# Two range checks moved from VectorE to ScalarE, and a re-planned order, in a fused attention and MLP kernel on one core

## The chip, the cores and the metric

One core of one Trainium2 chip runs one program. The metric is the device time of one execution in microseconds (us), taken as the median of several; lower is better. Engine names are those of the profile: PE (TensorE, its weight loads apart as PEld), DVE (VectorE), ACT (ScalarE), POOL (GpSimd), SP (the queue that issues the transfers).

## The reference

Three parts follow each other: a gated linear attention with complex gates, an RMS norm with a SiLU-gated MLP, and a second MLP with softplus. Cut to what matters (shapes: 4 x 8 heads x 768 steps x 48; 3072 tokens of 384; hidden widths 1536 and 2048):

```python
mag = np.sqrt(a_re * a_re + a_im * a_im)
scale = np.minimum(mag, 0.999) / (mag + 1e-06)
...
for t in range(S):
    new_re = ar * S_re - ai * S_im
    new_im = ar * S_im + ai * S_re
    kv = np.einsum('bhd,bhe->bhde', k[:, :, t], v[:, :, t])
    S_re, S_im = (new_re + kv, new_im)
    y[:, :, t] = np.einsum('bhd,bhde->bhe', q[:, :, t], S_re)
...
xn = x / rms * rms_g
g = xn @ w_gate
silu = g * (1.0 / (1.0 + np.exp(-g)))
return (silu * (xn @ w_val) @ w_out)
...
h = x @ w_in
g = np.maximum(h, 0.0) + np.log1p(np.exp(-np.abs(h)))
return (g @ w_out)
```

## The kernel before, in words

**Attention.** The 768 steps are cut into 6 chunks of 128 for each of 4 batches: 24 units. For each unit the gates' magnitudes and angles are formed (`squares`, `logs`, `mags`, `tangent`, `trigs`, `psi`, `frac`), q and k are scaled and rotated (`q_scaled`, `k_scaled`, `rotated`, tiles `pc` and `ps`), written to memory and read back in another layout (`relayout`, tiles `rot` and `QK`), and PE makes the products within a chunk (`gram`, L597; `ys`, L640 and L643; `kv`, L663; all in PSUM tiles `patt`). Two transposes and the RMS norm (`norm`, L710 to L714) give the unit's part of the first MLP's input, split into a rounded part `xh` and a rest `xl` (`x_evac`, L738 for `xl`). Most of this work is elementwise on tiles of 128x384, on DVE, ACT and POOL.

**The MLPs.** Each float32 product is made of three, rounded times rounded and the two cross terms, so each weight too is a pair (`w1h`, `w1l`). The first MLP works through 6 tiles of 512 tokens (4 units each) and 12 blocks of the hidden width: two input products (`a_in`, PSUM tile `hp`), SiLU on ACT (`sil`), a product with the gate on DVE, the split into `ph` and `pl` (L866), and an output product (`a_out`, PSUM tile `op`); all matmuls stand in L815. `ph` and `pl` have one buffer each, so a block's `ph` can be written only after the block before has been multiplied out. The second MLP has the same form (`b_in`, `b_act`, `b_out`).

**The weights** arrive as 64-bit numbers, in pieces of 128x384 (36 for the first MLP, 32 for the second). `w_split` makes float32 of each: ACT takes the high word's magnitude (L790) and the low word's bits (L792), DVE clamps the magnitude into a range (L795) and puts the bits together (L797 to L803), then the piece is split in two (`whi`, L808).

**Checks.** The fast path needs a gate's real part over a bound: L413 clamps it on DVE and accumulates the least value into `am`. Such checks meet in `flags` near the end of the attention; a flag that is set runs a general kernel instead.

**Order.** The program has no loop at run time. `Plan` holds every step with its cost on each engine that may do it (`CHOICE`), a position plus a correction from tables (`EARLY`, `LEAD`), and places them greedily on model clocks; the order of each engine's instructions is what comes out, and each engine then runs its list in that order. 150 matmuls without use (`keep_warm`, L1035) fill PE's gaps early on. The first `a_in` needs `xh` and `xl` of units 0 to 3.

Of the kernel before, what the change touches and what calls it, by code (L numbers as in the profile page):

```python
# [1301 lines left out]
```

## Time and profile before

| what | value |
|---|---|
| runs | 1105.39, 1106.09, 1109.11 us; median 1106.09 |
| the profiled execution's own time | 1107.23 us |
| its span, first to last instruction | 1105.4 us |
| PE, DVE, ACT, POOL busy | 1038.9, 781.7, 696.4, 167.8 us |
| first matmul of the first MLP | about 123.5 us after the start |

Busy times are of one execution. PE's is a modelled one, since matmuls overlap; an engine's busy share over the whole span mixes stages that have different limits, so the rows below are cut by stage.

### The profile page before, as it was taken

How to read it: one execution, taken by the hardware profiler on the slowest of the kernel's cores; microseconds unless marked ns; L12 is line 12 of the kernel's file. 1: busy time of each engine (PE TensorE's matmuls, PEld its weight loads, DVE VectorE, ACT ScalarE, POOL GpSimd, SP SyncE). 2: the span in 40 equal slices, each digit the busy share in tenths (PEclk: the TensorE clock that was granted, in tenths of full speed). 3: DMA queues.
4: the chain of work that ended last, by engine and by line, in shares of the span. 5: the costliest groups of instructions: out<-in, count | busy, mean ns of one | idle time of the engine just before them, and what ended most of it. 6: DMA issues, size and time to landing. Idle time of an engine off the chain costs nothing.

```text
span 1105.4 us, 15919 instructions
## 1 busy us (share of the span) xinstructions
PE 1038.9 (94%) x5694; PEld 873.5 (79%) x5694; DVE 781.7 (71%) x1541; ACT 696.4 (63%) x1275; POOL 167.8 (15%) x208
## 2 busy tenths in 40 slices
PE   0694899999999999999999999999999999999997
PEld 0693787888887888888888888888888888888886
DVE  7999999988999889898343298598445454544443
ACT  7797787688788788787422265596544454444543
POOL 1132312222334225232010000000000000000000
PEclk9996799999999999999999999999999999999999
DMA  6577556644565454453220054242001010000000
GB/s 197 153 198 173 164 151 168 157 137 112 143 138 136 121 146 108 139 142 93 79 73 20 20 152 115 72 137 63 29 1 58 1 58 1 10 29 1 29 1 32
DMA packets 98344, 103.84 MB, mean 94 GB/s; under 512 B 5456, under 2 KB 82640, under 8 KB 98256
## 3 DMA queue, kind: packets, MB, share of 16 engines
q1 hardware_dynamic: 98256, 102.73, 34.2%
q8 instruction: 47, 0.77, 0.3%
q14 instruction: 41, 0.34, 0.1%
HBM read 74.33 MB, written 28.39 MB: 93 GB/s over the span
## 4 chain that ended last, share of the span: by engine, by line
PE 74%; DVE 12%; ACT 6%; DMA 5%; issue 2%; POOL 1%; SPq 0%; ACTq 0%; DVEq 0%; POOLq 0%
PE hp L815 29%; PE op L815 27%; PE hq L815 7%; PE patt L597 3%; DMA QK<-rot 2%; PE patt L640 2%; PE op L1035 2%; PE patt L663 2%; ACT L1106 1%; DMA wst<-w 1%; DMA rot<-ps 1%; PE patt L643 1%; DVE pl L866 1%; PE patt L616 1%; DVE AT L607 1%
## 5 line engine op out<-in xcount | busy, mean ns | idle before, releaser
L815 PE MATMUL hp<-xh,w1h 128*128 128x512 f32 x516 | 207.4, 402 | 0.0
L815 PE MATMUL hp<-xl,w1h 128*128 128x512 f32 x516 | 201.9, 391 | 0.7 <-DVE xl L738 0.7
L815 PE MATMUL hp<-xh,w1l 128*128 128x512 f32 x516 | 202.0, 391 | 0.0
L815 PEld LDWEIGHTS hp<-xh,w1l 128*128 128x128 f32 x516 | 97.3, 188 | 21.0
L815 PEld LDWEIGHTS hp<-xl,w1h 128*128 128x128 f32 x516 | 97.5, 189 | 19.7 <-DVE xl L738 1.2
L815 PEld LDWEIGHTS hp<-xh,w1h 128*128 128x128 f32 x516 | 97.5, 189 | 19.0 <-issue 0.3
L962 DVE SCALAR_TENSOR_TENSOR be<-hp,be 128x512 f32<-128x512 f32 x58 | 40.1, 691 | 96.2 <-ACT be L959 96.2
L957 ACT ACTIVATE be<-hp 128x512 f32<-128x512 f32 x58 | 34.8, 600 | 104.6 <-PE hp L815 104.4
L863 DVE TENSOR_TENSOR sil<-sil,hp 128x512 f32<-128x512 f32 x72 | 49.0, 681 | 56.9 <-PE hp L815 53.4
L815 PE MATMUL op<-ph,w1h 128*128 128x512 f32 x216 | 87.0, 403 | 0.0
L815 PE MATMUL op<-pl,w1h 128*128 128x512 f32 x216 | 84.7, 392 | 0.2 <-DVE pl L866 0.2
L815 PE MATMUL op<-ph,w1l 128*128 128x512 f32 x216 | 84.4, 391 | 0.0
L372 ACT CAST ph<-sil 128x512 fp32r<-128x512 f32 x51 | 31.7, 621 | 67.5 <-PE op L815 37.1
L962 DVE SCALAR_TENSOR_TENSOR be<-hq,be 128x512 f32<-128x512 f32 x38 | 26.3, 692 | 63.8 <-ACT be L959 63.8
L866 DVE TENSOR_TENSOR pl<-sil,ph 128x512 fp32r<-128x512 f32 x72 | 56.0, 778 | 21.8 <-ACT ph L372 17.6
L965 DVE TENSOR_TENSOR bpl<-be,bph 128x512 fp32r<-128x512 f32 x96 | 66.3, 691 | 4.0 <-POOL bph L376 1.2
L597 PE MATMUL patt<-QK 96*128 96x128 f32 x384 | 52.2, 290 | 16.2 <-DMA QK<-rot 11.1
L597 PEld LDWEIGHTS patt<-QK 96*128 96x128 f32 x384 | 50.1, 203 | 20.5 <-issue 8.5
L1106 ACT ACT_TABLE_LOAD x51 | 65.4, 1283 | 0.7
L957 ACT ACTIVATE be<-hq 128x512 f32<-128x512 f32 x38 | 22.8, 600 | 67.5 <-PE hq L815 67.5
L855 ACT ACTIVATE sil<-hp 128x512 f32<-128x512 f32 x72 | 43.2, 600 | 32.4 <-PE hp L815 32.1
L958 ACT ACTIVATE be<-be 128x512 f32<-128x512 f32 x96 | 61.0, 635 | 3.0
(183 smaller groups left out, 2606.5 us busy)
## 6 DMA issues: line engine op xcount, KB each, us to landing
wst<-w SPq DMA_DIRECT2D x68, 384.0 KB, 3.2
QK<-rot SPq DMA_DIRECT2D x96, 192.8 KB, 4.9
rot<-pc SPq DMA_DIRECT2D x24, 385.5 KB, 3.3
rot<-ps SPq DMA_DIRECT2D x24, 385.5 KB, 4.2
aa<-aa SPq DMA_DIRECT2D x24, 384.0 KB, 4.2
qk<-qk SPq DMA_DIRECT2D x24, 384.0 KB, 5.3
v<-vv SPq DMA_DIRECT2D x24, 192.0 KB, 5.0
x2d<-ev SPq DMA_DIRECT2D x18, 256.0 KB, 2.6
```

The lines of the kernel that those rows point to most:

```text
L372: act.copy(out=dst, in_=src)
L597: pe.matmul(T(g)[:, i * C:(i + 1) * C], lhsT=T(q)[:, i, C:2 * C], rhs=T(q)[:, i, 0:C], start=True, stop=True)
L640: pe.matmul(o(h), lhsT=T(v)[:, h * D:h * D + 64], rhs=T(a)[:, h, :], start=True, stop=ch == 0)
L815: pe.matmul(o, lhsT=w[:, wcol + k * 128:wcol + (k + 1) * 128], rhs=x[:, k, 0:n], start=first and i == 0, stop=last and i == len(m) - 1)
L855: op(ACT, c_drain(n), lambda: act.activation(out=T(s)[:, 0:n], in_=T(g)[:, 0:n], func=AF.Silu), r=[g], w=[s, "silu"], prio=p, table="silu")
L863: op(DVE, c_dve(n), lambda: dve.tensor_tensor(out=T(s)[:, 0:n], in0=T(s)[:, 0:n], in1=T(v)[:, 0:n], op=ALU.mult), r=[v], w=[s], prio=p)
L866: flex("plo", "tt", n, lambda e: e.tensor_tensor(out=T(pl)[:, 0, 0:n], in0=T(s)[:, 0:n], in1=T(ph)[:, 0, 0:n].bitcast(F32), op=ALU.subtrac ...
L957: act.activation(out=T(e), in_=T(h), func=AF.Abs)
L958: act.activation(out=T(e), in_=T(e), func=AF.Exp, scale=-1.0)
L962: op(DVE, c_dve(512), lambda: dve.scalar_tensor_tensor(out=T(e), in0=T(h), scalar=0.0, in1=T(e), op0=ALU.max, op1=ALU.add), r=[h], w=[e], ...
L965: flex("bplo", "tt", 512, lambda x: x.tensor_tensor(out=T(pl)[:, 0], in0=T(e), in1=T(ph)[:, 0].bitcast(F32), op=ALU.subtract), r=[e, ph], ...
L1106: P.emit(lambda tab: tab in TABLES and act.preload_act_table_set(TABLES[tab]))
```

## The change

1. `squares`: the clamp of the gates' real part on DVE (L413) goes. Instead ACT forms relu(bound - value) and adds it up (`asum`), into the tile that the square of the real part then overwrites; a sum over zero sets the flag.
2. `w_split` for the first MLP's 36 pieces: DVE's clamp (L795) goes. ACT's magnitude step now adds up the magnitudes too, and a new ACT step (`w_small`) adds up relu(2^-15 - magnitude), writing into the place of the piece's later `w1h`. Both sums are compared in `flags`. The second MLP's pieces keep the clamp.
3. `flags` has 8 more small instructions on DVE; `floor` becomes one column, read 128 times over.
4. The planner: other waiting times from one engine to the next (`SEEN`), some other costs, `SLACK` 529 instead of 14578 (how much later than its best engine a step may end), other engines to choose from (`CHOICE`), and new numbers in `EARLY` and `LEAD`. Nearly every row of every engine's list moves.

```diff
+SEEN = {"dve": 115.0, "act": 140.0, "pe": 200.0, "pool": 140.0, "sp": 200.0, None: 200.0}
...
-    "bphi": "dp adp", "bplo": "p d", "add": "p d",
+    "bphi": "dp ad", "bplo": "d d", "add": "dp dp",
...
-    "whi": "ad adp", "wlo": "d d", "phi": "a ap", "plo": "d d", "oev": "a ad", "x2hi": "p adp", "x2lo": "d dp",
...
+    "whi": "adp ad", "wlo": "dp d", "phi": "a ad", "plo": "dp p", "oev": "a ad", "x2hi": "p dp", "x2lo": "dp dp",
...
-SLACK = 14578.0
+SLACK = 529.0
...
-                    ready[j] = max(ready[j], done + (GAP if self.ops[j][0][0][0] == e else 200.0))
+                    ready[j] = max(ready[j], done + (GAP if self.ops[j][0][0][0] == e else SEEN[e]))
...
 def c_pool2(n):
-    return 182 + 2.0 * n
+    return 260 + 2.0 * n
...
-        op(DVE, c_dve(N) + 60, lambda: dve.tensor_scalar(
-            out=T(k)[:, 0], in0=T(k)[:, 0], scalar1=AR_MIN, scalar2=None, op0=ALU.max, op1=ALU.min,
-            accum_out=am[:, u:u + 1]), w=[(k, 0), ("am", u)], prio=p)
+        op(ACT, c_act(N) + 50, lambda: act.activation(
+            out=T(a), in_=T(k)[:, 0], func=AF.Relu, scale=-1.0, bias=bias[:, 4:5], accum_out=am[:, u:u + 1]),
+            r=[(k, 0)], w=[a, ("am", u)], prio=p, name="asum")
...
-        op(POOL, 750, rstd, w=[ss], prio=p)
+        op(POOL, 1100, rstd, w=[ss], prio=p)
...
+    def w_abs(key, k, dst, dk, p):
+
+        if key[0] == "w2":
...
+        i = key[1]
+        op(ACT, c_act(PW, 0.5) + 50, lambda: act.activation(
+            out=dst(), in_=T(k)[:, :, 1].bitcast(F32), func=AF.Abs, accum_out=wm[:, 0, i:i + 1]),
+            r=[k], w=[dk, ("wb", i)], prio=p, name="w_abs")
+        op(ACT, c_act(PW) + 50, lambda: act.activation(
+            out=T(w1k[i // 3][0])[:, i % 3 * PW:(i % 3 + 1) * PW], in_=dst(), func=AF.Relu,
+            scale=-1.0, bias=bias[:, 5:6], accum_out=wm[:, 1, i:i + 1]),
+            r=[dk], w=[(w1k[i // 3][0], i % 3 * PW), ("ws", i)], prio=p, name="w_small")
...
-            op(ACT, c_act(PW, 0.5), lambda: act.activation(out=af(), in_=T(k)[:, :, 1].bitcast(F32), func=AF.Abs),
-               r=[k], w=[a], prio=p)
+            w_abs(key, k, af, a, p)
...
-            op(DVE, c_fast(PW), lambda: dve.tensor_scalar(
-                out=af(), in0=af(), scalar1=W_BIG, scalar2=2.0 ** -15, op0=ALU.min, op1=ALU.max), w=[a], prio=p, port=True)
...
+        if wide:
+            for i, limit, at in ((0, W_BIG, ALU.is_lt), (1, 0.0, ALU.is_le)):
+                dve.tensor_scalar(out=wm[:, i], in0=wm[:, i], scalar1=limit, scalar2=None, op0=at)
+                dve.tensor_reduce(out=fl[:, 3:4], in_=wm[:, i], axis=AX.X, op=ALU.min)
+                dve.tensor_scalar(out=fl[:, 3:4], in0=fl[:, 3:4], scalar1=1.0, scalar2=None, op0=ALU.is_lt)
+                dve.tensor_tensor(out=fl[:, 0:1], in0=fl[:, 0:1], in1=fl[:, 3:4], op=ALU.add)
...
-        op(DVE, 1500, flags, w=keys, prio=p)
+        op(DVE, 2300, flags, w=keys, prio=p)
```

Three places of the new order follow; the line numbers of the changed kernel are a little higher (L817 is L797 of before, L715 is L710, L886 is L866, L379 and L377 are L374 and L372, L883 is L863).

DVE at its first weight pieces (`ev` holds a piece's magnitude, `wst` its raw words, `aa` the gates), before:

```order
L795 TENSOR_SCALAR ev<-ev 128x384
L797 TENSOR_SCALAR ev<-ev 128x384
L800 SCALAR_TENSOR_TENSOR ev<-wst,ev 128x384
L795 TENSOR_SCALAR ev<-ev 128x384
L803 SCALAR_TENSOR_TENSOR ev<-ev 128x384
L797 TENSOR_SCALAR ev<-ev 128x384
```

and now:

```order
L817 TENSOR_SCALAR ev<-ev 128x384
L820 SCALAR_TENSOR_TENSOR ev<-wst,ev 128x384
L823 SCALAR_TENSOR_TENSOR ev<-ev 128x384
L817 TENSOR_SCALAR ev<-ev 128x384
L820 SCALAR_TENSOR_TENSOR ev<-wst,ev 128x384
```

Each piece has four rows here before, three now, and its first row now follows ACT's new step instead of ACT's magnitude step.

ACT around the norm square of unit 3, the last unit that the first MLP tile needs (`yx,ss<-patt` is that square, `wm` and `am` are the sums), before:

```order
L790 ACTIVATE ev<-wst 128x384
L792 ACTIVATE ev<-wst,bias 128x384
L366 ACTIVATE C<-C,mhalf 128x384
L790 ACTIVATE ev<-wst 128x384
L792 ACTIVATE ev<-wst,bias 128x384
L372 COPY yx<-patt 128x512
L386 ACTIVATE B<-aa 128x384
L710 ACTIVATE yx,ss<-patt 128x384
```

and now:

```order
L795 ACTIVATE ev,wm<-wst 128x384
L814 ACTIVATE ev<-wst,bias 128x384
L377 COPY yx<-patt 128x512
L798 ACTIVATE w1h_678,wm<-ev,bias 128x384
L715 ACTIVATE yx,ss<-patt 128x384
L391 ACTIVATE B<-aa 128x384
L377 CAST xh<-patt 128x3x128
L418 ACTIVATE A,am<-aa,bias 128x384
```

A piece has three rows on ACT instead of two (the third, L798, stands just ahead of the norm square), and the unit's gate sum (L418) is a row of ACT's.

POOL in the middle of the attention (`ph`, `pl` belong to the first MLP, `pc`, `qk`, `A`, `T`, `C` to the attention), before:

```order
L706 TENSOR_SCALAR ss<-ss 128x1
L708 TENSOR_TENSOR ss<-ss,mhalf 128x1
L418 TENSOR_TENSOR A<-A,B 128x384
L376 TENSOR_SCALAR pc<-e_all 128x3
L376 TENSOR_SCALAR ph<-sil 128x512
L376 TENSOR_SCALAR ps<-e_all 128x3
L376 TENSOR_SCALAR ph<-sil 128x512
L567 TENSOR_TENSOR pc<-qk,G 128x3x256
```

and now:

```order
L373 TENSOR_SCALAR T<-T 128x384
L474 TENSOR_TENSOR T<-aa,Z 128x384
L886 TENSOR_TENSOR pl<-sil,ph 128x512
L557 TENSOR_TENSOR qk<-qk,F 128x384
L498 TENSOR_TENSOR A<-B,C 128x384
L373 TENSOR_SCALAR C<-C 128x384
L886 TENSOR_TENSOR pl<-sil,ph 128x512
```

POOL now subtracts for `pl` (66 of its 72, all 72 of which were DVE's) and no longer makes `pc` (17, now DVE's); `ph` left POOL for DVE and ACT.

## Rows read from the trace of the kernel before

**Rows 1.** The page, parts 1 and 2: busy times, and PE's 40 slices.

```profile
PE 1038.9 (94%) x5694; PEld 873.5 (79%) x5694; DVE 781.7 (71%) x1541; ACT 696.4 (63%) x1275; POOL 167.8 (15%) x208
PE   0694899999999999999999999999999999999997
```

**Rows 2.** Windows by stage: length; PE, PEld, DVE, ACT, POOL busy; clock; DMA share, GB/s.

```profile
0.00:123.50 123.50, 69.06 (x548) 65.22 (x548) 110.74 (x253) 95.38 (x195) 29.84 (x35) 0.88 0.66 176
123.50:229.40 105.90, 103.26 (x630) 86.36 (x630) 101.16 (x219) 84.45 (x170) 24.92 (x26) 0.98 0.61 157
229.40:333.60 104.20, 103.99 (x653) 87.50 (x652) 94.44 (x178) 88.45 (x163) 30.86 (x43) 1.00 0.55 134
333.60:441.50 107.90, 106.73 (x694) 89.97 (x693) 94.06 (x181) 85.38 (x160) 43.59 (x47) 1.00 0.49 131
441.50:544.30 102.80, 102.20 (x634) 86.04 (x633) 81.30 (x149) 75.45 (x135) 24.21 (x32) 1.00 0.36 103
...
640.00:720.00 80.00, 80.00 (x354) 66.24 (x354) 60.71 (x134) 47.22 (x84) 1.75 (x3) 1.00 0.39 112
720.00:1092.00 372.00, 372.00 (x1642) 308.02 (x1642) 201.94 (x365) 194.19 (x321) 5.67 (x10) 1.00 0.10 31
```

**Rows 3.** The chain of waits, 0 to 140 us: start, length, what.

```profile
12.68 0.47 DVE w1l L808
...
17.75 0.28 DVE ev L795
...
26.91 0.27 DVE w1h L374
...
33.52 0.87 DVE pc L567
...
78.58 0.41 ACT A L386
...
93.18 0.52 ACT T L478 x2
...
104.61 6.64 DMA QK<-rot
...
124.42 0.47 DVE xl L738
```

**Rows 4.** Groups by line and shape: busy us and mean ns, then idle before.

```profile
L795 DVE TENSOR_SCALAR ev<-ev 128x384 f32<-128x384 f32 x68 | 26.1, 386 | 3.0 <-ACT ev L790 3.0
L413 DVE TENSOR_SCALAR_CACHE_REDUCE aa<-aa 128x384 f32<-128x384 f32 x24 | 12.9, 539 | 2.2 <-DMA aa<-aa 2.2
L478 ACT ACTIVATE T<-T 128x384 f32<-128x384 f32 x24 | 12.5, 522 | 0.4
L478 ACT ACTIVATION_READ_ACCUMULATOR T<-T 128x1 f32 x24 | 4.6, 191 | 0.0
```

**Rows 5.** The timeline around the flags, 586 to 588 us: start, length, what, idle before.

```profile
586.62 0.23 DVE L988 TENSOR_REDUCE fl<-e_all 128x1 f32<-128x72 f32 x1
...
587.50 0.17 DVE L996 MEMSET floor<- 128x128 f32 x1
```

**Rows 6.** The same stretch on PE.

```profile
587.81 0.35 PE L998 MATMUL patt<-fl,floor 128*128 128x3 f32 x2 [0.34 <-DVE floor L996]
```

**Rows 7.** Groups by line and shape: POOL's two-input work, and the split of the gated product.

```profile
L567 POOL TENSOR_TENSOR pc<-qk,G 128x768 f32<-128x768 f32 x17 | 32.3, 1898 | 28.5 <-ACT G L459 16.1 <-ACT pc L372 9.6 <-issue 2.5
...
L545 POOL TENSOR_TENSOR qk<-qk,E 128x384 f32<-128x384 f32 x8 | 17.2, 2151 | 46.4 <-DMA qk<-qk 29.4 <-DVE E L488 17.0
L418 POOL TENSOR_TENSOR A<-A,B 128x384 f32<-128x384 f32 x15 | 17.1, 1141 | 44.2 <-ACT A L386 41.0 <-DVE pl L866 3.1
```

**Rows 8.** The same view, where `ph` is made.

```profile
L372 ACT CAST ph<-sil 128x512 fp32r<-128x512 f32 x51 | 31.7, 621 | 67.5 <-PE op L815 37.1 <-DVE sil L863 29.1 <-DVE ev L797 0.6
```

**Rows 9.** The chain of waits past the attention.

```profile
600.54 2.04 PE hp L815 x9
602.58 2.04 PE op L815 x9
```

More of the change, by code (lines that the diff above doesn't have):

```diff
@@ new lines @@
+    "masked.dve": {0: -291, 1: -147, 2: -114, 3: -293, 4: 101},
+    "norm.act": {0: 400, 1: -226, 2: -473, 3: 340, 4: 281}, "norm.dve": {0: 32, 1: -139, 2: -192, 3: 321, 4: -347},
+    "norm.pool": {0: 199, 1: -29, 2: 477, 3: 46, 4: -36},
+    "nw1": {-1: 463, 0: 232, 1: -201, 2: 499, 3: -234, 4: -215},
+    "nw2": {-1: -328, 0: -73, 1: -268, 2: -453, 3: -307, 4: -374},
+    "nw3": {-1: -9, 0: -522, 1: 555, 2: -208, 3: -353, 4: 385}, "phi": {0: 142}, "plo": {0: 80},
+    "psi.dve": {0: 154, 1: 315, 2: 510, 3: 598, 4: 569}, "qe": {0: -453, 1: 492, 2: -180, 3: 385, 4: -476},
@@ new lines @@
+    "w_load.sp": {0: -315, 1: 129, 2: 392, 3: -44, 4: 491, 5: -219},
+    "w_small": {0: -397, 1: 145, 2: -12, 3: -329, 4: -96, 5: 214},
+    "w_split.act": {0: 255, 1: 482, 2: 106, 3: -480, 4: 380, 5: 309},
+    "w_split.dve": {0: 423, 1: 350, 2: 387, 3: -22, 4: 205, 5: -22},
+    "whi": {0: 179, 1: 445, 2: -139, 3: -158, 4: 47, 5: -302},
+    "wlo": {0: 369, 1: 204, 2: -291, 3: -243, 4: -514, 5: 75},
+    "x_evac.dve": {0: 342, 1: -300, 2: 227, 3: 95, 4: 101}, "x_tr.pe": {0: -404, 1: 95, 2: -342, 3: -163, 4: 68},
@@ new lines @@
+    "b_act.act": 431, "b_act.dve": -370, "b_in.pe": 318, "b_out.pe": -360, "back": -5, "begin_b.None": 151,
+    "bphi": -332, "bplo": 44, "carried.dve": -449, "carry": 119, "eend": -418, "evac.sp": -197, "flags.dve": 290,
+    "frac.dve": -83, "gram.pe": -389, "k_nat.pe": 184, "k_scaled.dve": 183, "kf": 301, "knev": -59, "kv.pe": -508,
+    "load_a.sp": -328, "load_consts.sp": -93, "load_qk.sp": 252, "load_v.pool": 345, "load_v.sp": 153, "logs2": -123,
+    "logs3": -40, "mags.dve": 198, "masked.dve": -165, "norm.act": -309, "norm.dve": 198, "norm.pool": -313,
@@ L324, in fused_kernel @@
     cst = ctx.enter_context(tc.tile_pool(name="cst", bufs=1, side="left"))
-    bias = cst.tile([128, 4], F32, name="bias")
+    bias = cst.tile([128, 8], F32, name="bias")
     mlp = ctx.enter_context(tc.tile_pool(name="mlp", bufs=1, side="left"))
@@ L342, in fused_kernel @@
     g_bc = ac.tile([128, DM], F32, name="g_bc")
-    floor = ac.tile([128, 128], F32, name="floor")
+    floor = edge.tile([128, 8], F32, name="floor")[:, 0:1]
     later_steps = ac.tile([128, N], F32, name="later_steps")
@@ L347, in fused_kernel @@
     am = ac.tile([128, NU], F32, name="am")
+    wm = ac.tile([128, 2, 3 * F1], F32, name="wm")
     zm = ac.tile([128, NU], F32, name="zm")
@@ L778, in w_load @@
             w=[k], prio=p, land=(1000, 1700))
+    def w_abs(key, k, dst, dk, p):
+        if key[0] == "w2":
+            op(ACT, c_act(PW, 0.5), lambda: act.activation(out=dst(), in_=T(k)[:, :, 1].bitcast(F32), func=AF.Abs),
+               r=[k], w=[dk], prio=p, name="w_abs")
+            op(DVE, c_fast(PW), lambda: dve.tensor_scalar(
+                out=dst(), in0=dst(), scalar1=W_BIG, scalar2=2.0 ** -15, op0=ALU.min, op1=ALU.max),
+                w=[dk], prio=p, port=True, name="w_clamp")
+            return
+        i = key[1]
[6 more added lines that the diff above has]
+            r=[dk], w=[(w1k[i // 3][0], i % 3 * PW), ("ws", i)], prio=p, name="w_small")
     def w_split(key, hi, lo, cols, p):
@@ L1041, in attention_done @@
         keys += [("e_all", u) for u in range(NU)]
+        keys += [(x, i) for x in ("wb", "ws") for i in range(3 * F1) if wide]
         tags = ("patt", "aa", "qk", "v", "A", "B", "C", "T", "Z", "E", "F", "G", "pc", "ps", "QK", "AT", "kn", "yx",
```

94 lines of the change are left out of this document (40 added, 54 removed), and 14 rows, old and new, of tables (CHOICE, EARLY).

## The prediction

> **What bounds the kernel now.** I read the page's busy times and slices first: PE is busy 94% of the span, and its slices are at nine tenths or more from the sixth to the last but one [rows 1]. A busy PE is a modelled one, so I then cut the span by stage: up to the first matmul of the first MLP (123.5 us), its first token tile (to 229.4), and the later ones [rows 2]. The reader is to see that PE is idle for 54.4 us of the first stage (and part of its 69.06 busy ones are the matmuls without use), 2.6 us in the next, and 0.2, 1.2 and 0.6 in the three that follow; from 640 us on it does not pause. Its useful work is the same before and after the change, so the end moves by what changes in PE's lost time, nearly all of which lies ahead of 123.5 us.
>
> Who sets that moment? DVE is busy 110.74 of 123.5 us (90%), ACT 95.38 (77%) [rows 2]. The chain of waits runs through DVE's list for most of the start, with one transfer in it (6.64 us for `QK`), and its last step before the first tile is DVE's `xl` of unit 3 at 124.42 us [rows 3]. DVE is the short engine at the start, and in tile 0 as well: 101.16 of 105.9 us (95.5%), against ACT's 84.45 (80%) [rows 2].
>
> **Prices.** A lone duration is longer than what an instruction adds to a full engine, so I take the chain's steps, where one follows another: 0.27 us for a clamp of 128x384, 0.27 for a cast or another one-input step, 0.47 for two inputs, 0.87 for the rotation of 128x768, 0.41 for a plain ACT step, 0.52 for one with the reading of its sum (the pair `x2`) [rows 3]. The groups give the lone ones: 386 ns for the clamp, 539 for the gates' clamp with its minimum, 522 plus 191 for ACT's step with its sum [rows 4]. The gates' clamp is a two-input step in length, 0.47. How a relu with a sum runs no row shows; the square with a sum is its nearest, 0.52 packed and 0.71 alone, and I take 0.52, since ACT's list is full here.
>
> **The start (to unit 3's `xl`).** I counted the rows of both orders ahead of that row on DVE. Gone: 19 clamps of weights (5.1 us) and 8 of gates (3.8). Come, by the new choices of engine: 12 one-input steps (3.2), 8 two-input ones (3.8), 2 weight casts (0.5), 2 `xh` (0.7), some 10 tiny ones (about 1); gone to others: 2 rotations (1.7) and 7 further steps (3.5). That is 4.9 us less. On ACT, up to unit 3's norm square: 7 gate sums (3.6), 19 new weight steps (9.9), 19 sums added to magnitude steps (0.1 each, 1.8), less some 20 steps that went to DVE and POOL (about 8): 7.1 us more. ACT then has 102.5 us to do in about 118.6, 86%: less than DVE's 90%. So DVE stays the gate, and what it loses the path loses: **-4.9 us**. Bounds: at an unchanged share of 90%, (110.7 - 4.9)/0.897 = 118.0, which is -5.5; and if unit 3's rotation gates instead, nearly nothing, for ahead of it DVE's list is only 0.3 us shorter.
>
> **Tile 0.** Between unit 3's and unit 7's `xl`, DVE loses 17 weight clamps (4.6), 3 of gates (1.4), 5 subtractions for `pl` (3.0) and gains 4.5 of others: -4.5, to 96.7 us of busy time. ACT gains 16 weight steps and 3 gate sums (9.9), 2 more magnitude steps and 17 sums (2.4), 2 table loads (2.6), less 1.0: +13.9, to 98.4 us, or 93% of a stage as long as before. The short engine changes from DVE to ACT. If ACT bears the 95.5% that DVE bore, the stage takes 98.4/0.955 = 103.0 us (-2.9); at 93% nothing changes; at 90% it takes 109.3 (+3.4). PE gives up to 2.6 us of idle time and some at its low clock (0.98 of full) [rows 2]. I take **-1.0**.
>
> The relu on ACT costs 0.52 us where DVE's clamp cost 0.27 [rows 3]. The Trainium skill, "ScalarE: Activation LUTs", section "Rules for kernel authors", says to put relu, max and min on VectorE; the trace agrees on the price of one, and by the rule alone the change loses 0.25 us for each weight piece. That counts only where ACT is the short engine, the rival (A) below.
>
> **From tile 1 on.** Of the rest of the attention DVE has 14 us less and ACT 10 us less, POOL 28 us more, since `pl` moves there. DVE's 94.44 of 104.2 us and ACT's 88.45 already let PE run with 0.2 us idle [rows 2]: little is to be had, 2.6 us at most over these stages. The cover of `pl` is PE's next block. After the attention a block's output product stands behind two input groups of 2.04 us each [rows 9], 4.08 us, in which `ph` (0.62) [rows 8] and `pl` must be made, with three hand-overs; one takes 0.14 us from the end of DVE's last flag row (587.67) to PE's start (587.81) [rows 5, 6]. POOL takes 1.14 us for two inputs of 128x384 and 1.90 for 128x768, so about 1.39 for 128x512; from its dearest group, 2.15 for 128x384, it would be 2.87 [rows 7]. That makes 2.4 to 3.9 us: covered, at the dear end only just. I take **-0.5**, bounds -2.6 and +2.
>
> **Flags.** Eight more small rows on DVE; eight such take 0.88 us now (586.62 to 587.50) [rows 5], and PE already waits 0.34 us behind them [rows 6]. No step covers it: **+0.9**.
>
> **The sum.** 1107.23 (profiled) - 4.9 - 1.0 - 0.5 + 0.9 = 1101.7; the median of the runs stands 1.1 us below the profiled one: **1100.6 us**. The likeliest case's own range is 1095.6 (all good bounds, -10.5) to 1105. About 0.3%, 3.3 us, is what a measurement here can tell from no change: faster means below 1102.8, slower above 1109.4.
>
> **Rivals.** (A) *Slower: ACT becomes the bound of tile 0.* Its new step stands ahead of DVE's first bit step of each piece, and DVE runs its list in order, so a late ACT also stops DVE, and units 4 to 7 come late for tile 1. It decides at a share of about 90%: there the loss eats the start's gain. At 85% the stage takes 98.4/0.85 = 115.8 us, +9.9, in all +5.9: 1112. For it: ACT held only 80% in this stage; against: it had no more work to do, and DVE held 95.5% beside it. 0.15.
>
> (B) *No change: the gain at the start is lost in waits.* Up to unit 3's rotation DVE's list is as long as before, and what is shorter after it is covered by the transfer to `QK` (6.64 us) [rows 3]. Then only the flags' +0.9 and small things stay: 1106 to 1107. 0.22.
>
> (C) *More: the re-planned order removes idle time as such.* DVE is idle for 12.8 us ahead of 123.5. If half of that goes too, -6: 1094 to 1095. For it: nearly every row has a new place, planned with other waits. Against: no row shows that the plan's waits were at fault. 0.14.
>
> (D) *`pl` on POOL comes late.* 16 of the 66 come after the attention; each 0.5 us late costs 8 us: 1108 to 1109. For it: the same two-input work takes POOL from 1.14 to 2.15 us on average [rows 7]. Against: DVE is busy only 60.71 of 80 us at its fullest there [rows 2]. 0.07. The Trainium skill, "SBUF — State Buffer", section "Who interferes with whom", has the cause: a DVE instruction with two inputs in SBUF and a POOL one that reads it exclude each other, the later one waiting to the end. The spread of POOL's groups agrees; by that rule POOL's 28 us more could also hold DVE by as much, 14 us more than it is freed, still under 96% of these stages.
>
> The forecast has 0.42. **Faster** 0.52 (0.36 of the forecast, 0.14 of C, 0.02 of B), **same** 0.28 (0.18 of B, 0.06 of the forecast, 0.04 of D), **slower** 0.20 (A 0.15, D 0.03, B 0.02). The range reaches to C and most of A: 1091 to 1111.
>
> **What would show it.** In the changed profile: the first matmul of `hp` at 117 to 120 us; DVE busy about 106 us ahead of it and ACT about 102; tile 0 from 103 to 106 us with ACT over 92% busy; PE's wait at the flags about 1.2 us; `pl` on POOL at 1.3 to 1.6 us with no pause of PE after 640 us. I am wrong if DVE sits idle for `w_small` for several us, if PE waits for `patt` work in tile 0, or if `pl` lasts over 2.5 us.

## The result, and the profile after

The changed kernel takes 1123.86 us (median of 4 runs, 1122.94 to 1124.7), the kernel before 1106.9 beside it: a ratio of 1.0144, 95% interval 1.0127 to 1.016. The forecast was 1100.6, within 1091 to 1111. It is 17.0 us slower. Executions of one program spread over some 5 us here: of the six of the run e1 below, three at a mean clock of 0.978 to 0.979 took 1113.8 to 1116.0 us and three at 0.984 to 0.985 took 1110.5 to 1110.9, and the changed kernel's four stand at 0.979 to 0.982.

The windows by stage, cut at the same matmuls as in [rows 2] as far as 344 us, and at 640.5 us, where the matmul stands that was at 632.8 before: length; PE, PEld, DVE, ACT, POOL busy; clock; DMA share, GB/s.

```profile
0.00:133.00 133.00, 70.17 (x548) 66.16 (x548) 109.03 (x245) 108.95 (x256) 32.92 (x37) 0.85 0.59 163
133.00:236.60 103.60, 102.70 (x631) 85.62 (x630) 97.52 (x200) 91.89 (x206) 34.65 (x34) 0.99 0.62 158
236.60:344.00 107.40, 105.94 (x687) 89.63 (x686) 91.57 (x163) 86.77 (x174) 45.28 (x52) 1.00 0.51 133
344.00:546.70 202.70, 202.70 (x1270) 171.11 (x1270) 156.49 (x280) 141.98 (x281) 80.82 (x85) 1.00 0.42 118
546.70:640.50 93.80, 91.55 (x513) 75.74 (x512) 41.38 (x85) 25.06 (x48) 22.95 (x26) 1.00 0.19 58
640.50:714.00 73.50, 73.50 (x325) 60.81 (x324) 56.35 (x102) 38.26 (x70) 16.84 (x15) 1.00 0.37 108
```

The span grew from 1105.4 to 1121.2 us, and the windows say where: the start +9.5 (123.5 to 133.0), the first tile -2.3 (105.9 to 103.6), all from there to 640.5 us +0.5, and +8.0 after the attention, where PE has no wait at all. The two big ones are one forecast with the wrong sign and one not forecast.

In the start, DVE and ACT are now busy for the same time, 109 us, and each only for 82% of it. The waits up to 133 us (engine and line that waited, for what; total us, times, longest):

```profile
PE patt L602 <- DMA QK<-rot: 15.7, 4, 7.0
DVE ev L817 <- ACT w1h L798: 4.3, 1, 4.3
DVE state L688 <- PE patt L668: 4.0, 5, 1.3
```

and the same three before, up to 123.5 us:

```profile
PE patt L597 <- DMA QK<-rot: 9.5, 2, 7.9
DVE ev L795 <- ACT ev L790: 3.0, 1, 3.0
DVE state L683 <- PE patt L663: 0.4, 1, 0.4
```

PE waits longer for the data of the grams (the products `gram` within a chunk). DVE waits once, at its first piece, for ACT's new step `w_small` (L798); it had waited there before, for the magnitude step, so only 1.3 us of this are new. And DVE waits longer for PE, whose clock stands at 0.85 on average (0.88 before). The groups of the new steps and of `pl` (busy us, mean ns):

```profile
L886 POOL TENSOR_TENSOR pl<-sil,ph 128x512 fp32r<-128x512 f32 x66 | 94.0, 1424 | 199.9 <-DVE ph L379 109.5 <-ACT ph L377 63.6 <-ACT pc L377 8.4
L798 ACT ACTIVATE w1h<-ev,bias 128x384 fp32r<-128x384 f32 x36 | 21.8, 606 | 0.0
L795 ACT ACTIVATE ev<-wst 128x384 f32<-128x384 f32 x36 | 19.7, 546 | 2.6 <-DMA wst<-w 2.6
L418 ACT ACTIVATE A<-aa,bias 128x384 f32<-128x384 f32 x24 | 14.8, 617 | 3.5 <-DVE E L493 1.9 <-DMA aa<-aa 1.4
L795 ACT ACTIVATION_READ_ACCUMULATOR ev<-wst 128x1 f32 x36 | 6.9, 191 | 0.0
L798 ACT ACTIVATION_READ_ACCUMULATOR w1h<-ev,bias 128x1 f32 x36 | 6.8, 190 | 0.0
```

The chain of waits has both sums at their packed price, 0.60 and 0.61 us; I had taken 0.52:

```profile
18.58 0.60 ACT w1h L798 x2
...
27.76 0.61 ACT A L418 x2
```

The flags (DVE's first and last row of the weights' eight, and PE behind them; those of before are [rows 5, 6]):

```profile
621.96 0.17 DVE L1016 TENSOR_SCALAR wm<-wm 128x36 f32<-128x36 f32 x1
...
623.28 0.16 DVE L1019 TENSOR_TENSOR fl<-fl 128x1 f32<-128x1 f32 x1
...
624.11 0.35 PE L1024 MATMUL patt<-fl,mask 128*128 128x3 f32 x2 [1.91 <-DVE mask L1022]
```

After the attention, the same 300 us of the second MLP hold 27 matmuls fewer. The window 760 to 1060 us, before:

```profile
760.00:1060.00 300.00, 300.00 (x1325) 248.43 (x1324) 147.75 (x248) 142.32 (x231) 3.10 (x5) 1.00 0.07 23
```

and after:

```profile
760.00:1060.00 300.00, 300.00 (x1298) 243.24 (x1297) 150.66 (x260) 146.36 (x242) 0.00 (x0) 1.00 0.08 25
```

That is 0.2264 and 0.2311 us for each, at a full clock and with PE always busy; 1728 matmuls lose 8.1 us. Before, every group of matmuls there has a mean of 389 ns, as

```profile
L815 PE MATMUL op<-bph,w1h 128*128 128x512 f32 x108 | 42.0, 389 | 0.0
```

After, it goes by operand:

```profile
L835 PE MATMUL op<-bph,w1h 128*128 128x512 f32 x114 | 45.1, 396 | 0.0
...
L835 PE MATMUL hp<-xl,w1h 128*128 128x512 f32 x66 | 25.7, 389 | 0.0
...
L835 PE MATMUL hq<-xh,w2h 128*128 128x512 f32 x45 | 17.9, 397 | 0.0
```

`w1h` and `xl` lie in pools on the left side of the memory, `w2h` and `bph` in one on the right, behind `edge`. `floor` is now a second tile of 32 bytes in `edge`, and in the built program all that lies behind it starts 32 bytes away from where it would: every tile of the second MLP's pool (`w2h`, `w2l`, `bph`, `bpl`) at 32 past a multiple of 64, where before they stood at multiples of 64, as `w1h`, `w1l`, `xh` and `xl` do in both. The groups with an operand from there (974 of the 1298) are longer, 391 to 397 ns, whichever of the two operands it is. Of the groups without one, those with `xl` stay at 389 and those with `xh` show 390 to 392; the records of neighbouring matmuls overlap (389 ns each, one every 226), so a group's mean is not one matmul's cost.

### The profile page after: what moved, and what is told of

Read it like the earlier page. It is cut to its first block, busy times and chain, and to the rows that moved or that the text cites. A ratio compares the mean times of both kernels' runs of the same rounds, so it can differ in the third digit from the quotient of the medians.

```text
span 1121.2 us, 16034 instructions
## 1 busy us (share of the span) xinstructions
PE 1047.0 (93%) x5694; PEld 873.5 (78%) x5694; DVE 770.0 (69%) x1466; ACT 704.7 (63%) x1389; POOL 233.9 (21%) x247
## 4 chain that ended last, share of the span: by engine, by line
PE 79%; DVE 7%; ACT 6%; DMA 5%; issue 2%; SPq 0%; POOL 0%; DVEq 0%; ACTq 0%; POOLq 0%
PE hp L835 32%; PE op L835 29%; PE hq L835 7%; PE patt L602 3%; DMA rot<-ps 2%; PE patt L668 2%; DMA QK<-rot 2%; PE patt L645 2%; PE patt L648 1%; DMA aa<-aa 1%; PE patt L621 1%; ACT L1135 1%; PE patt L698 1%; ACT L875 1%; DVE ev L820 1%
## 5 line engine op out<-in xcount | busy, mean ns | idle before, releaser
L886 POOL TENSOR_TENSOR pl<-sil,ph 128x512 fp32r<-128x512 f32 x66 | 94.0, 1424 | 199.9 <-DVE ph L379 109.5
L977 ACT ACTIVATE be<-hp 128x512 f32<-128x512 f32 x58 | 34.6, 597 | 108.1 <-PE hp L835 108.1
L883 DVE TENSOR_TENSOR sil<-sil,hp 128x512 f32<-128x512 f32 x72 | 49.2, 683 | 36.8 <-PE hp L835 28.9
L978 ACT ACTIVATE be<-be 128x512 f32<-128x512 f32 x96 | 60.7, 633 | 3.1
L979 ACT ACTIVATE be<-be 128x512 f32<-128x512 f32 x96 | 60.7, 632 | 3.1
```

The source lines that it names most:

```text
L883: op(DVE, c_dve(n), lambda: dve.tensor_tensor(out=T(s)[:, 0:n], in0=T(s)[:, 0:n], in1=T(v)[:, 0:n], op=ALU.mult), r=[v], w=[s], prio=p)
L886: flex("plo", "tt", n, lambda e: e.tensor_tensor(out=T(pl)[:, 0, 0:n], in0=T(s)[:, 0:n], in1=T(ph)[:, 0, 0:n].bitcast(F32), op=ALU.subtrac ...
L977: act.activation(out=T(e), in_=T(h), func=AF.Abs)
L978: act.activation(out=T(e), in_=T(e), func=AF.Exp, scale=-1.0)
L979: act.activation(out=T(e), in_=T(e), func=AF.Ln, bias=1.0)
```

## The experiments

All medians stand beside runs of the kernel before on the same chip. Old and new are the order and the checks of the kernel before and of the changed one; "PE kept busy" means more matmuls without use, told below. "First tile" is the time of the first matmul of the first MLP in the profiled execution (123.5 before, 133.0 changed), the busy times are those ahead of it. It is of one execution each: g3 and g5 are the same program up to the flags, and so are g4 and g6, and their first tiles begin at 119.3 and 122.2, and at 121.4 and 125.9 us. A difference of a few us in that column is no result by itself.

| run | order | the two checks | us | minus before | ratio, 95% | first tile | DVE, ACT busy |
|---|---|---|---|---|---|---|---|
| e1_one_edge_tile | new | new | 1112.35 | +6.5 | 1.0034-1.0077 | 131.9 | 109.1, 109.1 |
| e2_before_shifted | old | old | 1115.31 | +9.4 | 1.0055-1.0095 | 124.4 | - |
| e4_sums_not_issued | new | none | 1107.59 | +1.7 | 1.0007-1.0031 | 125.8 | 107.5, 92.8 |
| e5_after_order_old_checks | new | old | 1115.58 | +8.0 | 1.0049-1.0096 | 135.2 | 118.0, 91.5 |
| e8_before_no_clamps | old | none | 1105.34 | -2.3 | 0.9964-0.999 | 126.4 | 102.5, 95.0 |
| e9_before_order_new_checks | old | new | 1119.77 | +12.2 | 1.0089-1.0136 | 127.9 | 102.6, 113.3 |
| e7_relu_constant_bias | new | new | 1112.15 | +6.3 | 1.0034-1.0067 | 128.6 | 108.2, 105.0 |
| e10_flags_rows_early | new | new | 1116.39 | +8.8 | 1.006-1.0094 | 132.7 | 108.1, 107.0 |
| e11_sum_not_tied | new | new | 1115.56 | +8.0 | 1.0048-1.0102 | 128.3 | 108.0, 107.0 |
| f1_before_more_warm | old, PE kept busy | old | 1107.22 | -0.4 | 0.9978-1.0008 | 122.7 | 110.9, 95.3 |
| f2_no_clamps_more_warm | old, PE kept busy | none | 1100.73 | -6.9 | 0.9909-0.9953 | 118.5 | 102.1, 94.9 |
| f3_after_mended | new, PE kept busy | new | 1113.67 | +6.1 | 1.0028-1.007 | 129.9 | 109.1, 106.7 |
| g1_before_order_new_checks_warm | old, PE kept busy | new | 1120.23 | +13.3 | 1.0074-1.0144 | 130.0 | 103.0, 113.5 |
| g2_after_order_no_checks_warm | new, PE kept busy | none | 1106.93 | 0.0 | 0.9961-1.0003 | 127.1 | 107.0, 92.5 |
| g5_weights_late | old, PE kept busy | gates old | 1110.45 | +2.3 | 1.0002-1.0032 | 122.2 | 106.5, 96.5 |
| g6_weights_late_gate_sum | old, PE kept busy | gates new | 1115.16 | +7.0 | 1.0039-1.0079 | 125.9 | 102.0, 100.4 |

**The shifted operands.** First the changed kernel with one tile in `edge`:

```diff
-    mhalf = edge.tile([128, 8], F32, name="mhalf")[:, 0:1]
+    edge_t = edge.tile([128, 8], F32, name="mhalf")
+    mhalf, floor = edge_t[:, 0:1], edge_t[:, 1:2]
...
-    floor = edge.tile([128, 8], F32, name="floor")[:, 0:1]
```

> The changed kernel, with `floor` as a second column of the tile of `mhalf` instead of a tile of its own. No instruction and no order changes; only the tiles of the right-hand pools, among them the second weights and their products `bph` and `bpl`, go back by 32 bytes, to a multiple of 64. Theory: the 8.4 us that the changed kernel loses after 700 us, where each matmul takes 0.2316 us instead of 0.2267, come from that shift: then 0.2267 again and about 1115.4 us. Rival: they come from what the other engines do beside PE in the new order: then 0.2316 and about 1123.9 us.

and the kernel before with a wider tile there:

```diff
-    mhalf = edge.tile([128, 8], F32, name="mhalf")[:, 0:1]
+    mhalf = edge.tile([128, 16], F32, name="mhalf")[:, 0:1]
```

> The kernel before, with the tile of `mhalf` 16 numbers wide instead of 8; everything else is as it was, and no instruction moves in any engine's list. The tiles of the right-hand pools then start 32 bytes higher, as in the changed kernel. Theory (the place of the matmuls' operands sets their time): each of the 1728 matmuls after 700 us takes 0.2316 instead of 0.2267 us, about +8.4, so about 1115 us, and nothing changes ahead of 700 us. Rival (the new order sets it): 1106.9 us as before.

The window 760 to 1060 us of the changed kernel with one tile:

```profile
760.00:1060.00 300.00, 300.00 (x1325) 248.43 (x1324) 152.59 (x263) 149.54 (x247) 0.00 (x0) 1.00 0.07 24
```

and of the kernel before with the wide one:

```profile
760.00:1060.00 300.00, 300.00 (x1298) 243.17 (x1297) 145.98 (x246) 139.26 (x228) 3.10 (x5) 1.00 0.06 23
```

Both ways as the theory said: 32 bytes take or give the 27 matmuls, with no instruction moved. By the differences to before this is 10.5 us (17.0 - 6.5) in one and 9.4 in the other. The second is the better figure, since three of e1's six executions stand at a higher clock than any of the changed kernel's. Some 8 us of it fall in the second MLP. What is left of the change is +6.5 us; all further runs have the shift undone.

**Checks and order apart.** Four runs keep one order exactly and swap the checks. In the changed order neither sum is issued (both range checks left out):

```diff
-        op(ACT, c_act(N) + 50, lambda: act.activation(
-            out=T(a), in_=T(k)[:, 0], func=AF.Relu, scale=-1.0, bias=bias[:, 4:5], accum_out=am[:, u:u + 1]),
+        op(ACT, c_act(N) + 50, lambda: None,
...
-        op(ACT, c_act(PW) + 50, lambda: act.activation(
-            out=T(w1k[i // 3][0])[:, i % 3 * PW:(i % 3 + 1) * PW], in_=dst(), func=AF.Relu,
-            scale=-1.0, bias=bias[:, 5:6], accum_out=wm[:, 1, i:i + 1]),
+        op(ACT, c_act(PW) + 50, lambda: None,
```

> As the run with one edge tile, but the two new ACT steps (the relu sums of the gates and of the weights) are not issued, so these two range checks are left out; the plan and the order of all the rest are as in the changed kernel. Theory 1: these steps and their hand-overs to DVE hold the start: the first matmul of the first MLP, at 133.0 us in the changed kernel, comes at 121 to 125, and the time falls by 8 to 11 us against that run, to about 1105. Theory 2: the re-planned order itself holds it (the first gates' load behind the constants, unit 4's work ahead of the first block): the first matmul stays at 129 or later, and the time falls by less than 4 us.

In the old order, no clamps for gates and first weights:

```diff
-        op(DVE, c_dve(N) + 60, lambda: dve.tensor_scalar(
+        op(DVE, c_dve(N) + 60, lambda: None, w=[(k, 0), ("am", u)], prio=p)
...
-            op(DVE, c_fast(PW), lambda: dve.tensor_scalar(
-                out=af(), in0=af(), scalar1=W_BIG, scalar2=2.0 ** -15, op0=ALU.min, op1=ALU.max), w=[a], prio=p, port=True)
+            op(DVE, c_fast(PW), lambda: dve.tensor_scalar(
+                out=af(), in0=af(), scalar1=W_BIG, scalar2=2.0 ** -15, op0=ALU.min, op1=ALU.max) if key[0] == "w2" else None, w=[a], prio=p, port=True)
```

> The kernel before with its own order, but DVE's clamps of the gates and of the first weights are not issued, so both range checks are left out; every other row of every engine's list stands where it stood. 27 DVE rows worth 8.9 us by the prediction's prices (0.27 and 0.47 us each) are gone ahead of the first matmul of the first MLP. Theory of the prediction (DVE is the gate at the start, and what it loses the path loses): that matmul comes at 115 to 119 us instead of 123.5, and the time is about 1099. Rival (the start is a net of hand-overs in which DVE's list is only one strand): it comes less than 3 us earlier, and the time is 1103 to 1106.

The old order with the new checks in place of the clamps:

```diff
+        def asum_square(e):
+            act.activation(out=T(a), in_=T(k)[:, 0], func=AF.Relu, scale=-1.0, bias=bias[:, 4:5], accum_out=am[:, u:u + 1])
+            square(e, T(a), T(k)[:, 0])
...
+                act.activation(out=af(), in_=T(k)[:, :, 1].bitcast(F32), func=AF.Abs, accum_out=wm[:, 0, i:i + 1])
+                act.activation(out=T(hi)[:, cols], in_=af(), func=AF.Relu, scale=-1.0, bias=bias[:, 5:6],
+                               accum_out=wm[:, 1, i:i + 1])
```

> The order of before with the new checks: DVE's clamps are gone, the two relu sums stand on ACT right ahead of the gates' square and right behind the weights' magnitude step, the magnitudes are added up, and the flags have their 8 rows more. Nothing else moves. Theory 1 (ACT's new steps hold the start whatever the order): the first matmul of the first MLP comes about 6 us later than without checks in this order, as it did in the changed order (131.9 against 125.8), and the time is 5 us over that run. Theory 2 (the changed order is the harm, and its new steps only hurt there): it comes within 2 us of the run without checks, and the time is under 1106.

The changed order with the old clamps where the sums stood:

```diff
+        op(ACT, c_act(N) + 50, lambda: dve.tensor_scalar(
+            out=T(k)[:, 0], in0=T(k)[:, 0], scalar1=AR_MIN, scalar2=None, op0=ALU.max, op1=ALU.min,
+            accum_out=am[:, u:u + 1]),
...
+        op(ACT, c_act(PW) + 50, lambda: dve.tensor_scalar(
+            out=dst(), in0=dst(), scalar1=W_BIG, scalar2=2.0 ** -15, op0=ALU.min, op1=ALU.max),
```

> The changed kernel's order (one edge tile) with the checks of before: DVE clamps where ACT's two relu sums stood, the magnitudes are not added up, the flags are as before. It tells what the order alone does. Theory 2 (the order is the harm): the first matmul of the first MLP at 129 us or later, the time 1110 or more. Theory 1 (ACT's new steps are the harm): it comes at 122 to 127 us and the time is within 2 us of 1107, as where neither check is issued. By the prediction's step (DVE is the gate) it would come 8.9 us later than without checks, at about 134.

Against before, with old, no and new checks, the old order stands at 0, -2.3 and +12.2, the new one at +8.0, +1.7 and +6.5. So the new checks by themselves cost 12 us in an order that was not made for them, and the re-planned order gives half of that back; without checks it is itself 4 us worse than the old one. Each order is best with no checks; the old one is far better with the old checks than with the new, while in the new order the two lie 1.5 us apart, with intervals that overlap. The old checks in the new order (e5) are a place where the prediction's step held: 10.5 us more on DVE than without checks (118.0 against 107.5) put the first tile 9.4 us later, at 135.2, where 134 was expected. In the changed kernel the two sums cost 4.8 us (1112.35 to 1107.59), between my two theories, of which neither held alone. The old order without clamps was the surprise: DVE has 8 us less to do, and 2.3 come of it, as the rival had it and not the prediction's step. (Its profiled execution took 1107.88 us, 2.5 over its median, and the first tile at 126.4 is of that one.)

Not all of e9's loss is in the start. In its profile the first tile begins 4.4 us later than before, and the second MLP 11.5 later (715.9 against 704.4). In tile 0, taken here to the first matmul of tile 1, ACT is the fuller engine too: 95.91 of 106.5 us against DVE's 94.97, where before it had 82.66 of 104.1 against 100.34. Theory 1 had the time's direction, but not the place: the first tile comes 1.5 us later than e8's, not 6.

**Small things in the new order.** The constant bias:

```diff
-            scale=-1.0, bias=bias[:, 5:6], accum_out=wm[:, 1, i:i + 1]),
+            scale=-(2.0 ** 15), bias=1.0, accum_out=wm[:, 1, i:i + 1]),
```

> As the run with one edge tile, but both relu sums are taken of 1 - value/bound instead of bound - value, so that the bias is the constant 1 and no column of a tile is read for it; the order is unchanged. Theory: the column costs about 0.09 us of the 0.60 that a step adds to a full ACT, the step falls to 0.52, the price of the prediction, and with 26 of them ahead of the first matmul it comes 1 to 2.5 us earlier. Rival: the price is that of the relu, and nothing moves.

The group of `w_small` falls from 606 ns to 516 (the scale changes with the bias),

```profile
L798 ACT ACTIVATE w1h<-ev 128x384 fp32r<-128x384 f32 x36 | 18.5, 516 | 0.0
```

but the time does not (+6.3 against +6.5). The flags' rows moved ahead:

```diff
+            for j, limit, at in ((0, W_BIG, ALU.is_lt), (1, 0.0, ALU.is_le)):
+                dve.tensor_scalar(out=wm[:, j], in0=wm[:, j], scalar1=limit, scalar2=None, op0=at)
+                dve.tensor_reduce(out=wf[:, j:j + 1], in_=wm[:, j], axis=AX.X, op=ALU.min)
```

> As the run with one edge tile, but the comparison of the weights' sums (six small DVE rows now) stands right behind the last weight sum, in the first MLP's first tiles, and the flags at the end of the attention have only one row more than before. Theory: PE's wait at the flags' matmul falls from 1.91 us to about 0.5, and the time by 1.4 us, from 1112.3 to about 1111. Rival: the wait moves to the next step behind the flags, and the time does not change.

```profile
624.67 0.35 PE L1034 MATMUL patt<-fl,mask 128*128 128x3 f32 x2 [0.58 <-DVE mask L1032]
```

PE's wait falls by 1.3 us; the time is not lower (intervals overlap), so of this only the wait is shown. The sum untied from the weights:

```diff
-            out=T(w1k[i // 3][0])[:, i % 3 * PW:(i % 3 + 1) * PW], in_=dst(), func=AF.Relu,
-            scale=-1.0, bias=bias[:, 5:6], accum_out=wm[:, 1, i:i + 1]),
+            out=T(w1k[i // 3][0])[:, i % 3 * PW:(i % 3 + 1) * PW], in_=later_steps, func=AF.Relu,
+            scale=-1.0, bias=bias[:, 3:4], accum_out=wm[:, 1, i:i + 1]),
```

> As the run with one edge tile, but the weights' relu sum reads a constant tile instead of the piece's magnitude (so the lower bound of the weights is not looked at), with the same size, engine and place in ACT's list. DVE's first bit step no longer waits for it; only its time on ACT stays. Theory of hand-overs (DVE stands idle for this step): most of the 4.8 us that the two sums cost in this order come back, 1107 to 1109. Theory of occupancy (ACT's list is longer, and whatever stands behind is late): 1111 to 1113, unchanged.

DVE's wait for `w_small` is gone,

```profile
DVE ev L817 <- ACT ev L795: 3.2, 1, 3.2
```

and now stands at the magnitude step ahead of it. No gain (+8.0; the intervals of e11 and e1 overlap): the theory of hand-overs fails. That it is the step's time on ACT that costs fits this, but the four executions spread from 1111.0 to 1118.8 us and do not show it by themselves.

**PE's clock.** In the run of the old order without clamps, PE is busy for 8 of 13 us from 84 us on, and then has its low level of 1.2 GHz until past the first tile's begin (windows 84 to 97, 97 to 118 and 118 to 132 us):

```profile
84.00:97.00 13.00, 8.02 (x63) 7.16 (x62) 11.02 (x23) 9.31 (x22) 1.00 (x1) 0.87 0.62 143
97.00:118.00 21.00, 8.59 (x39) 7.33 (x41) 18.30 (x37) 15.54 (x33) 6.41 (x8) 0.51 0.90 197
118.00:132.00 14.00, 11.79 (x54) 9.64 (x55) 12.07 (x28) 8.96 (x21) 1.82 (x5) 0.51 0.44 125
```

and DVE waits 11.0 us for PE's grams (L595) and products (L661):

```profile
DVE AT L605 <- PE patt L595: 8.9, 6, 4.1
...
DVE state L681 <- PE patt L661: 2.1, 4, 0.7
```

where before, with a clock of 0.51 from 97 to 118 us too, it waits 3.8 us for the grams and 0.4 for the products (shown above):

```profile
DVE AT L607 <- PE patt L597: 3.8, 4, 1.6
```

Three runs put matmuls without use where PE had waited there (the table shown is that of the old order; f3 has one of its own, of 84, and later g1 has the first and g2 the second):

```diff
+    WARM = {('gram', 2): 16, ('y_nat', 2): 4, ('x_tr', 2): 9, ('gram', 3): 32, ('x_tr', 3): 6}
+
+    def more_warm(*key):
+        for _ in range(WARM.pop(key, 0)):
+            pe.matmul(T(later["fill"])[:, 0:128], lhsT=ident, rhs=ident, start=True, stop=True)
```

> The kernel before in its own order, with 67 more matmuls without use (0.21 us each) on PE, put where PE waited in the profile between 84 and 122 us: 16 ahead of the grams of unit 2, 4 ahead of its first transposes, 9 ahead of its last ones, 32 ahead of the grams of unit 3, 6 ahead of its last transposes. Theory 3 (PE's clock is a strand of the start: it is granted at half for some 30 of the 40 us ahead of the first tile, and the grams and transposes that the other engines wait for take twice as long): the clock stays at full until the first tile, whose first matmul comes 3 to 6 us earlier, and the time is 1101 to 1104. Rival: nobody waits for PE there, and the time is within 1 us of the kernel before, or above it by the matmuls added.

> As the run of the kernel before without DVE's clamps (both range checks left out), with the same 67 matmuls without use. It tells whether DVE's 8.9 us less were lost to PE's clock. If so, this run is 3 to 6 us below the one with the matmuls and the clamps, about 1098. Rival (DVE's list is not what holds the start, clock or no clock): within 1.5 us of that run.

> The changed kernel's order with all that the runs so far suggest: one edge tile, the constant bias in both relu sums, the weights' flag rows early, and 84 matmuls without use where PE waited between 86 and 131 us. Theory 3: the first matmul of the first MLP at about 123 to 126 us (131.9 with one edge tile alone), and the time is 1103 to 1107. Rival (the clock is not a strand): about 1110.5, as the sum of the small things gives.

Without clamps and with these matmuls (same windows, same waits):

```profile
84.00:97.00 13.00, 10.77 (x102) 9.85 (x101) 12.02 (x24) 10.49 (x22) 3.55 (x4) 1.00 0.47 132
97.00:118.00 21.00, 16.49 (x148) 15.07 (x146) 19.77 (x42) 14.20 (x33) 5.30 (x10) 1.00 0.91 194
118.00:132.00 14.00, 12.42 (x54) 9.85 (x54) 14.00 (x28) 13.89 (x28) 5.21 (x4) 0.88 0.66 189
```

```profile
DVE AT L612 <- PE patt L602: 3.4, 3, 1.8
...
DVE state L690 <- PE patt L670: 1.0, 3, 0.5
```

The clock alone gives nothing (f1, -0.4, with 0.85 in place of 0.51 from 97 to 118 us), which refutes f1's theory; DVE's shorter list alone gives 2.3, both together 6.9 (f2), and the first tile begins at 118.5 us. DVE and PE's clock hold the old order's start together: of DVE's 8 us, 6.8 more went into waits for a PE at half its clock (11.0 us in e8's profile against 4.2 before), and with the clock kept, without clamps, these waits are 4.4. In the changed order with its checks (f3) the clock brings nothing (+6.1 against e7's +6.3), which fell short of my theory.

**What the sums cost when the clock is kept.**

> The order of before with the new checks, and the 67 more matmuls without use. With the clock kept, the same order took 1107.2 us with DVE's clamps and 1100.7 without any check of these two. Theory 1 (the two relu sums on ACT cost more than the clamps they replace, clock or no clock): above 1107, some 1111 to 1117, as 12 us of loss without the matmuls suggest. Rival (the loss was the clock's): below 1107, as the prediction had it.

> The changed order with one edge tile, neither of the new ACT steps issued (both range checks left out), and 84 more matmuls without use. Without these matmuls it took 1107.6 us. If the clock takes the gain of a shorter list in this order too, 1102 to 1104; if the changed order is bound by its own hand-overs, within 1.5 us of 1107.6.

The new checks in the old order, up to the first tile and through it:

```profile
0.00:130.00 130.00, 79.76 (x681) 75.82 (x681) 102.97 (x220) 113.46 (x267) 25.26 (x35) 0.97 0.61 167
130.00:239.50 109.50, 103.50 (x628) 86.07 (x629) 95.74 (x196) 97.95 (x227) 23.91 (x26) 0.98 0.59 152
```

and no check there:

```profile
0.00:118.50 118.50, 77.12 (x682) 73.87 (x682) 102.14 (x218) 94.86 (x196) 29.18 (x36) 1.00 0.70 183
```

ACT has 18.6 us more, and the first tile comes 11.5 us later. Theory 1 holds, with more loss than it had. DVE's longest wait with the new checks in this order is for ACT's step with the gates' sum (L416), 8.5 us in g1 and 7.2 in e9, and is not among its waits without checks; in e9:

```profile
DVE A L389 <- ACT A L416: 7.2, 3, 3.0
```

So at 87% busy ACT is now the engine that the start waits for, and through the first tile too it does more than DVE (97.95 us against 95.74). Of the 14.6 us by which the second MLP begins later than in f1 (718.1 against 703.5), 7.3 stand ahead of the first tile.

The changed order without checks gains less from a kept clock: g2 is 1.7 us below e4 by the differences of the medians, some 4 by the ratios, whose intervals do not overlap; the old order without checks gained 4.6. What stands in its way was not found.

Last, the weights' check late and weaker: DVE reduces the finished pieces behind the products of tiles 1 to 3.

```diff
+            w = T(w1k[i // 3][0])[:, i % 3 * PW:(i % 3 + 1) * PW].bitcast(F32)
+            dve.tensor_reduce(out=wm[:, 1, i:i + 1], in_=w, axis=AX.X, op=ALU.min, apply_absolute_value=True)
```

> What the runs point to: the order of before; the gates' clamp stays on DVE; the weights' clamp goes; instead DVE takes the least magnitude of each finished piece of `w1h` in one reduction, one behind each of 36 gate products in the first MLP's tiles 1 to 3, and ACT's magnitude step adds up the magnitudes for the upper bound; the flags get one row more; 67 more matmuls without use. DVE loses 5.1 of the 8.9 us ahead of the first tile, and ACT gains 1.8 there. Theory (DVE's list and the clock are together what holds the start): 1102 to 1104.5. Rival (the late reductions on a DVE that is 90% busy in those tiles, or ACT's sums, take it back): 1106 or more.

> As the run with the weights checked late, but the gates' clamp goes too, and ACT's relu sum (constant bias) stands in its place, one for each of the 24 units. It prices the gates' half of the change alone: DVE loses 3.8 us more ahead of the first tile, ACT gains 8 steps of 0.52. If DVE's time is worth more there than ACT's, 1 to 2.5 us below the run with the gates' clamp; if a step on ACT costs what it cost in the runs with both sums, 2 us or more above it.

These two compared with a bound for raw words, raised the flag, and ran the general kernel (17953 and 17959 us): their times tell nothing here, though up to the flags they are the programs of the next two. With the other bound:

> As the run with the weights checked late, with the bound that belongs to finished weights (2^-126; the other bound belongs to the raw words, finished weights lie below it, so the flag was set and the general kernel ran). The look is weaker than before: a raw word out of range that comes out as another value is not seen. DVE loses 5.1 of the 8.9 us ahead of the first tile, ACT gains 1.8, PE's clock is kept. Theory (DVE's list and PE's clock hold the start together): 1102 to 1104.5. Rival (the 36 late reductions or ACT's sums take it back): 1106 or more.

> As the other run of this call, with ACT's relu sum of the gates (constant bias, one for each unit) in place of DVE's clamp. It prices the gates' half of the change alone. DVE loses 3.8 us more ahead of the first tile, ACT gains 8 steps of 0.52 there. If a step on ACT costs about one for one, as the run with all new checks in this order says: 1 to 4 us above the other run; if DVE's time is what counts: 1 to 2.5 us below it.

The first is a miss (+2.3), and the rival holds. A late reduction takes 543 ns of DVE in its group, where the clamp's group had 386 [rows 4], and tiles 1 to 3, where the reductions stand, take 324.5 us in its profile (228.8 to 553.3) against f1's 319.0 (226.9 to 545.9):

```profile
L888 DVE TENSOR_REDUCE wm<-w1h 128x1 f32<-128x384 f32 x36 | 19.6, 543 | 0.0
```

The second prices the gates' half by itself: 4.7 us over the first, with intervals that do not overlap. Ahead of the first tile DVE has 4.5 us less and ACT 3.9 more, and that tile begins 3.7 us later (122.2 to 125.9), or 2.1 in the pair g3 and g4 (119.3 to 121.4). No version with both checks beat the kernel before.

## Why the prediction was wrong, point by point

**Nothing from 640 us on.** The first step that failed is "Its useful work is the same before and after the change, so the end moves by what changes in PE's lost time". The work is the same, but not its price: I costed the new tile `floor` at nothing, because no instruction of the second MLP changes, and 1728 matmuls went from 0.2264 to 0.2311 us each without a wait. That is the largest single error: 9.4 to 10.5 us of 17.0, shown both ways.

**The start, -4.9.** It came out at +9.5 in the profile. The second step that failed is "ACT then has 102.5 us to do in about 118.6, 86%: less than DVE's 90%. So DVE stays the gate, and what it loses the path loses". Three things were wrong in it. The share of 90% was taken as what an engine can bear, when it was reached beside an ACT at 77%; with both at 109 us each reaches 82%, and the stage takes 133. DVE had 109.03 us, not 106, and ACT 108.95, not 102 (part of it that the stage is longer; a sum took 0.60 and not 0.52). And PE's clock was not in the sum: with it kept, and no ACT step in exchange, DVE's 8.8 us (110.9 to 102.1) are worth 6.5 (f1 to f2), three quarters of what the step says; with the clock as it was, 2.3. The exchange itself is a loss, by 4.7 us for the gates alone. And the re-planned order adds to it: without any check its first tile is no earlier than before (125.8 us), and its time 1.7 us longer.

**Tile 0, -1.0.** It took 103.6 us, -2.3, inside its bounds, with ACT at 89% and not over 92.

**From tile 1 on, -0.5, and flags, +0.9.** Together +0.5 where I had +0.4, which is luck in part: the flags were sized too small, and the rest gained about 1.1 where I had 0.5. `pl` on POOL took 1.42 us, within 1.3 to 1.6, and PE did not pause after 640 us. (The dear price of 2.15 us was the mean of eight rows of which one took 6.7 us and one 3.4, the other six 1.0 to 1.3; what made these two long is not shown.) The flags' wait grew by 1.57 (0.34 to 1.91): the eight rows took 1.5 us, not 0.88. Four at a time each read what the one before wrote, and they start 0.19 to 0.22 us after one another, where the three small rows ahead of them, which do not, start 0.06 to 0.07 apart. Two slips in the sums (ACT's list in the start adds up to 7.3 and not 7.1, the good bounds to -10.1 and not -10.5) carry nothing.

**The rivals.** (A) had the right engine, ACT, and the right cause, its dearer step, in the wrong stage: tile 0 gained, the start lost. In the old order the same checks cost in both (e9, g1). The rule of the Trainium skill, "ScalarE: Activation LUTs", section "Rules for kernel authors", that relu belongs on VectorE, agrees with these runs (the gates' relu on ACT instead of DVE's clamp: +4.7 us). I had let the price count only where ACT is the short engine, and did not see that the change makes it as full as DVE (109 us each). (B)'s mechanism, waits that eat a shorter list, is what the old order without clamps showed, though the waits were for PE at its low clock and not for the transfer. (D) did not happen. (C), a better order as such, is refuted: without checks the new order is 4 us worse (e4, e8), 6 to 7 with the clock kept (g2, f2). It is better than the old one only under the new checks (+6.5 against +12.2).

**Open.** Why the changed order gains nothing from a kept clock with its checks and less than the old one without, and what in it costs those 6 to 7 us, was not settled. Nor was the split of the +6.5 into start and later stages, since a start stands in one profile each. Why a shift of 32 bytes lengthens a matmul is not shown either, only that it does.

## What to carry to other kernels

When a tile is added to a pool, ask which operands of later matmuls lie behind it, and compare matmuls per window before and after. Two engines that hand each other work may not both reach the share that one bore beside a less busy one (here 82% each, not 90%): price a moved step also as if it stood on the path of the engine that takes it. Where a start waits for PE in short pieces, look at its granted clock before counting on what another engine gives up.

## What the runs showed of the hardware

In a full stream of float32r matmuls of 128x512, three quarters of them with one operand or both at 32 past a multiple of 64 bytes in the partition, a matmul took 0.2311 us on average, against 0.2264 with all operands at multiples of 64 (1298 and 1325 in 300 us), at the same full clock. A bias read from a column of a tile cost an ACT step of 128x384 about 90 ns (606 and 617 ns against 516 and 526 with a constant bias and another constant scale).
